# Re-laying the side work of a fused channel-attention and SwiGLU kernel over its pipeline steps

## The chip, the cores and the metric

The kernel runs on one core of one Trainium2 chip. The metric is device time in microseconds (us), from three timed runs before the change: 1446.28, 1451.61 and 1455.15, median 1451.61. A profile shows one further execution of 1448.67 us, whose span from the first to the last instruction is 1446.8 us. Engines are named as in the profile: PE is the matrix engine (PEld its weight loads), DVE the vector engine, ACT the scalar engine, POOL is GpSimd, SP issues the DMAs.

## What is computed

Two batches of 6016 rows and 256 channels go through a channel attention; its output, read as 12032 tokens of 256, goes through a gated feed-forward layer of width 1536.

```python
qn = q / (norm(q, axis=1) + 1e-06);  kn = k / (norm(k, axis=1) + 1e-06)
s = kn.transpose(0, 2, 1) @ qn / tau
a = exp(s - s.max(-1)); a /= a.sum(-1) + 1e-09     # "quotients"
x = (v @ a).reshape(12032, 256)
xn = x / sqrt(mean(x * x, -1) + 1e-06) * rms_g
g = xn @ w_gate;  silu = g / (1 + exp(-g))
out = (silu * (xn @ w_val)) @ w_out
```

## The kernel before

All matrix products of the feed-forward part are kept near fp32 accuracy by splitting each operand into a high part (rounded to a shorter type, "hi", made on ACT) and a low part (the rest, "lo", a subtraction on DVE or POOL), and adding three products: hi·hi, hi·lo, lo·hi.

The 12032 tokens are worked off in 24 blocks j = 0 to 23 of up to 512 tokens, each block in 12 steps f = 0 to 11 of 128 hidden columns. Blocks 2 to 22 use a Winograd form of Strassen's scheme, seven products for eight. The seven products of step (j, f) are spread over three calls of `emit_step`: numbers 5 and 1 in the step itself, 3 and 6 one step later, 7, 2 and 4 two steps later. So in each step PE does products 7 and 2 of two steps ago (tiles `pu`, `pq`), 3 and 6 of the step before, 5 and 1 of this step, then the first half of an output job (`po`, five steps late), product 4 of two steps ago, and the second half of the output job. A step's `pu` tile is one of three; its `pq` is the only one.

The chain behind the products runs over two steps. In an even step DVE adds the gate products (L801, L802), ACT makes the Silu (L817, L835); in the odd step DVE adds the value products (L801, L802), multiplies (L820, then L829 after product 4), ACT makes the hi part `gx` (L734) and POOL its lo part (L740). For column pairs 1 to 4 of a block ("turned" pairs) DVE then makes four differences in place in the same tile `zg` (`run_turned`, L726), in the next even step, once POOL has read it; one step later ACT and POOL make `gy` and `gz` from the differences.

Output jobs of a block accumulate in four banks `po0` to `po3`. `po2` lies in the bank of pool `ps_m`, `po3` in that of `ps_s`; the two halves of the attention product `px` of a later block use the same two banks.

Beside this main chain, each block j carries side work for other blocks, which three tables lay over its steps: `steady` (after the step), `steady_mid` (inside the step, before the output halves) and `steady_pre` (before the Silu or the multiply). `turn4`, `turn3`, `turn2` are the same for blocks 4, 3 and 2. Within an engine the order is the order in which the code is written; each engine works its own list strictly in that order. The names in the tables:

- for block j-1: `copy` (ACT, one accumulator's copy, L1011), `sums_` (DVE, four adds, L1021), `c0`, `c1` (DVE, L1030), `store` (DVE transposes, L1041, and four DMAs);
- for block j+1: `scale` (ACT, L558, waits for 16 DMAs issued after `m1`), `parts` (POOL, L571 and L576), `xh0`, `xh1` (ACT, hi parts, L600), `xl0`, `xl1` (DVE, lo parts, two instructions each, L612);
- for block j+2: `v1` (DVE transposes, L427), `vh1`, `vl1` (hi and lo of v, L443, L448), `x0`, `x1` (PE, `px`, L459), `q0`, `q1` (ACT squares, L475), `r0`, `r1` (POOL, two small instructions, L484 and L488), `n0`, `n1` (ACT, L500, reads `px` and `r`'s result and so sets its bank free), `m0`, `m1` (DVE transposes, L539; behind `m1` the 16 DMAs on SP, L548);
- for block j+3: `load` (4 DMAs), the first half's transposes, hi (`split_v_high`) and later lo (`vl0`).

Of the kernel before, what the change touches and what calls it, by code (L numbers as in the profile page):

```python
# [12 lines left out]
ALU = mybir.AluOpType  # L13
# [6 lines left out]
def kernel(  # L20
# [17 lines left out]
    nc = tc.nc  # L38
# [3 lines left out]
    KC = C // P  # L42
# [6 lines left out]
    STRA = 4  # L49
# [43 lines left out]
    def f32(ap):  # L93
        return ap.bitcast(F32)
# [210 lines left out]
    def softmax_div(b, c):  # L305
        if c == 0:
            a_hl[b] = []
            for i in range(2):
                a_hl[b].append(sm_p.tile([P, KC, C], F32R, tag=f"a{i}", name=f"a{i}_{b}"))
                if b == i == 0:  # L310
                    sm_p.tile([P, 8], F32, tag="apart", name="apart")
        ah, al = a_hl[b]
        z, mx = sm_t[b]
        s = mx[:, KC + c:KC + c + 1]
        nc.vector.tensor_scalar(out=s, in0=s, scalar1=1e-9, scalar2=None, op0=ALU.add)
        nc.vector.reciprocal(s, s)
# [23 lines left out]
    B1 = NB // B  # L340
# [219 lines left out]
    def emit_xT_parts(j):  # L560


        if j == NB - 1:
            return
        h = blocks[j][2] * P // 2
        x = moved[j]
        new_xT(j)
        t = xn_p.tile([P, 4, HN], F32, tag="moved", name=f"xp_{j}")
        moved[j] = (x, t)
        a2, b2 = (x[:, 1, i * h:(i + 1) * h] for i in range(2))  # L570
        nc.gpsimd.tensor_tensor(  # L571
            out=t[:, 0:3:2, :h], in0=x[:, :, h:2 * h],
            in1=x[:, 0, :2 * h].rearrange("p (i n) -> p i n", i=2), op=ALU.subtract,
        )
        for o, i0 in ((1, b2), (3, a2)):
            nc.gpsimd.tensor_tensor(out=t[:, o, :h], in0=i0, in1=t[:, o - 1 if o == 1 else 1, :h], op=ALU.subtract)  # L576

    def xT_round(j, i):

        h = blocks[j][2] * P // 2  # L580
        slots = ((0, 1), (1, 3)) if i == 0 else ((3, 5), (5, 7))
        hi, lo = ([y[:, a:b] for a, b in slots] for y in xp[j])
        if i == 0:
            x = [moved[j][0][:, c, :2 * h].rearrange("p (i n) -> p i n", i=2) for c in range(KC)]
            src = [x[0][:, :1], x[1]]
        else:
            src = [moved[j][1][:, m:m + 2, :h] for m in (0, 2)]
        return src, hi, lo

    def emit_xT_high(j, i):  # L590
        if j == NB - 1:
            if i == 0:
                new_xT(j)
                nc.scalar.activation(
                    out=xT[j][0], in_=moved[j][:, :, :blocks[j][2] * P], func=AF.Copy
                )
            return
        src, hi, _ = xT_round(j, i)
        for o, x in zip(hi, src):
            nc.scalar.activation(out=o, in_=x, func=AF.Copy)  # L600

    def emit_xT_low(j, i, engine=nc.vector):
        if j == NB - 1:
            if i == 0:
                nc.vector.tensor_tensor(
                    out=xT[j][1], in0=moved[j][:, :, :blocks[j][2] * P], in1=f32(xT[j][0]),
                    op=ALU.subtract,
                )
            return
        src, hi, lo = xT_round(j, i)  # L610
        for o, x, y in zip(lo, src, hi):
            engine.tensor_tensor(out=o, in0=x, in1=f32(y), op=ALU.subtract)  # L612

    def emit_xT_round(j, i):
        emit_xT_high(j, i)
# [38 lines left out]
    def build_so(k, piece):  # L654
        p = PAIRS[k]
        if piece == 0:
            t = s_tmp["so", k] = pool["wk"].tile([P, 4, 2 * P], F32, tag="wk", name=f"wo_{k}")
            nc.vector.tensor_tensor(
                out=t[:, :2], in0=f32(wo[0][:, 2 * p:2 * p + 2]), in1=f32(wo[1][:, 2 * p:2 * p + 2]),
                op=ALU.add,  # L660
            )
            a12, a22, a11, a21 = (t[:, i, e * P:(e + 1) * P] for i in range(2) for e in range(2))
            s1, s2, s3, s4 = (t[:, 2 + i, e * P:(e + 1) * P] for i in range(2) for e in range(2))
            for o, i0, i1, op in (
                (s1, a21, a22, ALU.add), (s2, s1, a11, ALU.subtract),
                (s3, a11, a21, ALU.subtract), (s4, a12, s2, ALU.subtract),
            ):
# [386 lines left out]
    with tc.manual_schedule():  # L1054
# [42 lines left out]
        for i in range(nch):  # L1097
            n = chunks[0][i][1]
# [89 lines left out]
        def at(j, f, go):  # L1188
            extra.setdefault((j, f), []).append(go)
# [75 lines left out]
            at(STRA - 1 + f // NF, f % NF, lambda k=k, i=i: build_so(k, i))  # L1265
        at(STRA, 7, last_so)
        for i in range(3):
            at(STRA, 7 + i, lambda i=i: build_so(3, i))

        at(3, 1, lambda: inverse_norms(1))  # L1270
        at(3, 2, lambda: spread_norms(1, ps_m, "m"))
# [1 line left out]
        at(3, 5, lambda: softmax_min(1, 0))  # L1273
        at(3, 6, lambda: softmax_min(1, 1))
        at(7, 4, lambda: (softmax_exp(1, 0), softmax_exp(1, 1)))
        at(B1 - 2, 2, lambda: softmax_div(1, 0))
        at(B1 - 2, 3, lambda: softmax_div(1, 1))

        steps = [(j, f) for j in range(NB) for f in range(NF)]
        owed = []  # L1280
# [49 lines left out]
        vh0, vl0, vh1, vl1 = (of(2, lambda n, go=go, h=h: go(n, h)) for h in range(2) for go in (split_v_high, split_v_low))  # L1330
        xh0, xl0, xh1, xl1 = (of(1, lambda n, go=go, i=i: go(n, i)) for i in range(2) for go in (emit_xT_high, emit_xT_low))

        steady = {
            0: (scale, vl0),
            1: (xh0, v1),
            2: (sums_, xl0),
            3: (vh1, xh1),
            4: (c0, c1, vl1),
            5: (store, xl1),
            6: (n0,),  # L1340
            7: (r1, load),
            8: (m0,),
            10: after(3, vm(0)),
            11: after(3, lambda n: split_v_high(n, 0)),
        }
        steady_mid = {1: (parts,), 2: (copy,), 4: (x0, q0, r0), 6: (x1, q1)}
        steady_pre = {8: (n1,), 9: (m1,)}
        turn4 = {
            **steady,
            0: (vl0,),  # L1350
            1: (scale, v1),
            2: (xh0,),
            3: (xl0, xh1),
            4: (vh1, c0, c1),
            5: (vl1,),
            6: (store, n0, xl1),
        }
        turn4_mid = {**steady_mid, 1: (), 2: (parts,), 4: (lambda j: build_so(2, 2), x0, q0, r0)}
        turn3 = {
            3: (v0,),  # L1360
            4: (c0, c1, scale, s0),
# [2 lines left out]
            7: (s1,),  # L1364
            8: (rest, load),
            9: (n0,),
            10: (r1,),
            11: (m0, m1, *after(3, vm(0)), *after(3, lambda n: split_v_high(n, 0))),
        }
        turn3_mid = {5: (parts,), 7: (x0, q0, r0), 9: (x1, q1), 11: (n1,)}  # L1370
        turn2_mid = {**turn3_mid, 0: after(1, xn(1)), 5: ()}
# [4 lines left out]
            5: (scale,),  # L1376
            6: (parts, hi, v1),
            8: (rest,),
            11: (m0, m1),
        }  # L1380
        turn1 = {
            0: after(1, vs(1), sq(0), rr(0)),
# [22 lines left out]
        }  # L1405
        ends = (turn0, turn1, turn2, turn3, turn4, steady)
        mids = ({}, {}, turn2_mid, turn3_mid, turn4_mid, steady_mid)
        pres = ({}, {}, {}, {}, steady_pre, steady_pre)

        def emit_all(o):  # L1410
            go = emit_out(*o)
# [77 lines left out]
```

## Time and profile before

| | before |
|---|---|
| median of three runs | 1451.61 us |
| profiled execution, its span | 1448.67 us, 1446.8 us |
| PE busy, share of the span | 1310.4 us, 91% |
| DVE, ACT, POOL busy | 985.3 us (68%), 857.2 us (59%), 653.2 us (45%) |
| mean granted PE clock | 0.976 of full speed |
| block 13 (one of the like blocks 5 to 20), its length | 58.28 us |

PE is busy 91% of the span, but its ends are modelled, and a busy PE may run at half its clock. So a block is best read by its length, by where PE's idle time stands in it, and by the clock there.

### The profile page before, as it was taken

What the parts mean: (1) busy time and instruction counts of PE and PEld (TensorE: products, weight loads), DVE (VectorE), ACT (ScalarE), POOL (GpSimd) and SP (SyncE); (2) the same over time, 40 slices, a digit from 0 to 9 for tenths busy, and PEclk for the clock granted to TensorE, in tenths of its full rate; (3) what the DMA queues carried; (4) which work ended last, traced back from release to release, by engine and by line L of the source; (5) the groups of instructions that cost most, each with busy time, mean ns of one, the idle gap of its engine ahead of it and who ended that gap; (6) DMA issues with size and microseconds to landing.
All of it is one profiled execution on the core that took longest, in us unless ns stands there. A gap on an engine that the chain in (4) does not pass through costs nothing.

```text
span 1446.8 us, 25348 instructions
## 1 busy us (share of the span) xinstructions
PE 1310.4 (91%) x9312; PEld 1225.9 (85%) x9312; DVE 985.3 (68%) x1746; ACT 857.2 (59%) x1765; POOL 653.2 (45%) x531
## 2 busy tenths in 40 slices
PE   9999999988898888988889889898898898988999
PEld 7899899978798787887888879888788798887998
DVE  5799786668667756667666666776666666766663
ACT  5566566666555665655556655566565555565652
POOL 0210466645454454444545445446354554454450
PEclk9999999999999999999999999999999999999999
DMA  8975311202102111021020210211102102111121
GB/s 290 309 238 153 95 44 29 32 15 45 30 16 43 23 24 30 15 45 30 15 35 14 41 30 16 43 22 25 31 15 45 30 16 39 21 27 16 25 60 27
DMA packets 229373, 75.98 MB, mean 53 GB/s; under 512 B 186880, under 2 KB 220800, under 8 KB 229248
## 3 DMA queue, kind: packets, MB, share of 16 engines
q1 hardware_dynamic: 228416, 73.12, 21.3%
q8 instruction: 73, 1.20, 0.3%
q10 hardware_dynamic: 832, 1.25, 0.3%
q14 instruction: 52, 0.43, 0.1%
HBM read 48.50 MB, written 14.42 MB: 43 GB/s over the span
## 4 chain that ended last, share of the span: by engine, by line
PE 26%; ACT 11%; DVE 9%; POOL 9%; issue 5%; SPq 4%; DMA 1%; DVEq 0%; POOLq 0%; ACTq 0%
PE pu L772 12%; PE po L996 9%; POOL gz L740 4%; SPq L548 4%; DVE xt L612 4%; POOL gx L740 2%; ACT t L813 2%; ACT zg L817 2%; PE pq L772 2%; POOL gy L740 1%; ACT xn L475 1%; PE px L459 1%; DVE zg L801 1%; ACT xnT L558 1%; DMA xnT<-xw 1%
## 5 line engine op out<-in xcount | busy, mean ns | idle before, releaser
L772 PE MATMUL pu<-xt,w 128*128 128x256 f32 x2268 | 401.4, 286 | 22.0 <-DVE zv L801 16.6
L772 PE MATMUL pu<-xt,s 128*128 128x256 f32 x2268 | 366.3, 286 | 20.2 <-ACT zg L835 10.7
L772 PEld LDWEIGHTS pu<-xt,w 128*128 128x128 f32 x2268 | 330.2, 192 | 47.4 <-DVE zv L801 29.1
L772 PEld LDWEIGHTS pu<-xt,s 128*128 128x128 f32 x2268 | 316.6, 192 | 42.4 <-ACT zg L835 18.4
L740 POOL TENSOR_TENSOR gy<-zg,gy 128x512 fp32r<-128x512 f32 x126 | 172.1, 1366 | 282.1 <-ACT gy L734 239.1
L740 POOL TENSOR_TENSOR gx<-zg,gx 128x768 fp32r<-128x768 f32 (+1 forms) x126 | 205.5, 1631 | 207.9 <-ACT gx L734 129.8
L813 ACT ACTIVATE t<-pu 128x512 f32<-128x512 f32 x252 | 151.1, 600 | 176.0 <-DVE zg L802 80.5
L996 PE MATMUL po<-gx,w 128*128 128x256 f32 (+1 forms) x984 | 191.5, 315 | 0.0
L726 DVE TENSOR_TENSOR zg<-zg 128x256 f32<-128x256 f32 x304 | 129.0, 424 | 88.3 <-POOL gx L740 80.5
L808 ACT ACTIVATE t<-pu 128x256 f32<-128x256 f32 x252 | 96.1, 381 | 99.0 <-PE pu L772 98.6
L734 ACT ACTIVATE gx<-zg 128x768 fp32r<-128x768 f32 (+1 forms) x126 | 96.0, 762 | 83.9 <-DVE zg L829 61.2
L996 PEld LDWEIGHTS po<-gx,w 128*128 128x128 f32 x984 | 141.0, 189 | 4.5
L820 DVE TENSOR_TENSOR zg<-zg,zv 128x768 f32<-128x768 f32 x126 | 135.8, 1078 | 10.0 <-ACT zg L817 0.3
L801 DVE TENSOR_TENSOR zv<-pu,t 128x512 f32<-128x512 f32 x126 | 85.8, 681 | 70.2 <-PE pu L772 56.3
L772 PE MATMUL pq<-xt,w 128*128 128x256 f32 x756 | 132.6, 285 | 0.0
L996 PE MATMUL po<-gy,so 128*128 128x256 f32 x342 | 68.9, 315 | 64.4 <-ACT xn L500 64.4
L801 DVE TENSOR_TENSOR zg<-pu,t 128x512 f32<-128x512 f32 x126 | 86.4, 686 | 46.5 <-POOL gz L740 30.9
L740 POOL TENSOR_TENSOR gz<-zg,gz 128x512 fp32r<-128x512 f32 x76 | 116.2, 1528 | 0.0
L996 PEld LDWEIGHTS po<-gy,so 128*128 128x128 f32 x342 | 55.7, 215 | 68.1 <-ACT xn L500 68.1
L772 PEld LDWEIGHTS pq<-xt,w 128*128 128x128 f32 x756 | 110.1, 194 | 0.0
L817 ACT ACTIVATE zg<-zg 128x768 f32<-128x768 f32 x126 | 105.8, 840 | 0.0
L185 PE MATMUL s<-raw 128*128 128x256 f32 x376 | 87.3, 386 | 3.2 <-DMA raw<-in_k_dram 3.2
(173 smaller groups left out, 2204.9 us busy)
## 6 DMA issues: line engine op xcount, KB each, us to landing
v<-in_v_dram SPq DMA_DIRECT2D x84, 128.0 KB, 3.8
xnT<-xw SPq DMA_DIRECT2D x336, 32.0 KB, 1.9
out_dram<-ob SPq DMA_DIRECT2D x84, 128.0 KB, 3.3
raw<-in_q_dram SPq DMA_DIRECT2D x20, 512.0 KB, 5.0
raw<-in_k_dram SPq DMA_DIRECT2D x19, 512.0 KB, 6.4
wraw<-in_moe_w_gate_dram SPq DMA_DIRECT2D x12, 256.0 KB, 5.3
wraw<-in_moe_w_val_dram SPq DMA_DIRECT2D x12, 256.0 KB, 5.5
wraw<-in_moe_w_out_dram SPq DMA_DIRECT2D x12, 256.0 KB, 5.7
```

Source lines behind the costliest of these rows:

```text
L185: nc.tensor.matmul(out=s_ps[b][:, c, :], lhsT=r[:, 1, t, c * P:(c + 1) * P], rhs=r[:, 0, t, :], start=(t0 + t == 0 and c == 0), stop=(t0 + ...
L548: nc.sync.dma_start(out=x[S * i:S * (i + 1), :, a * n * S:(a + 1) * n * S], in_=w[S * a:S * (a + 1), :, i, :n, :].rearrange("p c t s -> p ...
L726: nc.vector.tensor_tensor(out=z[:, o], in0=z[:, i0], in1=z[:, i1], op=ALU.subtract)
L734: nc.scalar.activation(out=gh, in_=hh, func=AF.Copy)
L740: engine.tensor_tensor(out=gl, in0=hh, in1=f32(gh), op=ALU.subtract)
L772: nc.tensor.matmul(out=out, lhsT=wm[wi], rhs=xm[xi], start=(start and q == 0), stop=(q == 2), skip_group_check=True,)
L801: nc.vector.tensor_tensor(out=z[:, 1:], in0=u, in1=t[:, :2], op=ALU.add)
L808: nc.scalar.activation(out=mt[:, 0], in_=mu[:, 1], func=AF.Copy)
L813: nc.scalar.activation(out=nt[:, 1:], in_=nu, func=AF.Copy)
L817: nc.scalar.activation(out=zg[:, 1:], in_=zg[:, 1:], func=AF.Silu)
L820: nc.vector.tensor_tensor(out=zg[:, 1:], in0=zg[:, 1:], in1=z, op=ALU.mult)
L996: nc.tensor.matmul(out=acc[b][:, o:o + g.shape[-1]], lhsT=w, rhs=g, start=first, stop=True, skip_group_check=True,)
```

## The change

The tables are laid anew for blocks from 4 on. The halves of `px` and what follows them (`x`, `q`, `r`, `n`) stand a step earlier, and `n1` two steps; `copy` stands behind step 2 instead of inside it; `scale`, `xl0`, `vl1` and `store` move into the middle of later steps; `xh1` goes from behind step 3 to behind step 5, and `xl1`, two instructions behind step 5, is split into one inside step 7 and one behind it. In block 4 the side work moves further (its `scale` from behind step 1 into step 3, `n1` into step 8), and a weight preparation of that block goes two steps later. The first half's hi part moves ahead of `gx` in step 11. Batch 1's quotients (`softmax_div`) are made behind steps 9 and 11 of block 9 instead of 2 and 3 of block 10. `new_xT` is called where the first hi part is made. No arithmetic instruction is added or dropped.

```diff
-        new_xT(j)                       # emit_xT_parts
 ...
     def emit_xT_high(j, i):
+        if i == 0:
+            new_xT(j)
 ...
-    def emit_xT_low(j, i, engine=nc.vector):
+    def emit_xT_low(j, i, engine=nc.vector, part=None):
 ...
+        for k, (o, x, y) in enumerate(zip(lo, src, hi)):
+            if part in (None, k):
+                engine.tensor_tensor(out=o, in0=x, in1=f32(y), op=ALU.subtract)
 ...
-            at(STRA, 7 + i, lambda i=i: build_so(3, i))
+            at(STRA, 9 + i, lambda i=i: build_so(3, i))
 ...
-        at(B1 - 2, 2, lambda: softmax_div(1, 0))
-        at(B1 - 2, 3, lambda: softmax_div(1, 1))
+        at(B1 - 3, 9, lambda: softmax_div(1, 0))
+        at(B1 - 3, 11, lambda: softmax_div(1, 1))
 ...
+        xl1a, xl1b = (of(1, lambda n, k=k: emit_xT_low(n, 1, part=k)) for k in range(2))
         steady = {
-            0: (scale, vl0),
+            0: (vl0,),
             1: (xh0, v1),
-            2: (sums_, xl0),
-            3: (vh1, xh1),
-            4: (c0, c1, vl1),
-            5: (store, xl1),
-            6: (n0,),
-            7: (r1, load),
+            2: (copy, sums_),
+            3: (vh1,),
+            4: (c0, c1),
+            5: (xh1,),
+            7: (xl1b, load),
             8: (m0,),
             10: after(3, vm(0)),
-            11: after(3, lambda n: split_v_high(n, 0)),
         }
-        steady_mid = {1: (parts,), 2: (copy,), 4: (x0, q0, r0), 6: (x1, q1)}
-        steady_pre = {8: (n1,), 9: (m1,)}
+        steady_mid = {
+            1: (scale,),
+            2: (parts, xl0),
+            3: (x0, q0, r0),
+            4: (vl1, n0),
+            5: (x1, q1, r1),
+            6: (n1, store),
+            7: (xl1a,),
+            9: (m1,),
+            11: after(3, lambda n: split_v_high(n, 0)),
+        }
```

On POOL, block 14, from the lo part of pair 0's second half (`gy1_14_1`) in step 5 on; `ss` and `rr` of `16_1` are `r1`, on which `n1` waits. Before:

```order
L740 TENSOR_TENSOR gy1_14_1_10149<-zg_14_0_10068,gy0_14_1_10148 128x512
L740 TENSOR_TENSOR gx1_14_2_10259<-zg_14_2_10169,gx0_14_2_10258 128x768
L740 TENSOR_TENSOR gy1_14_3_10261<-zg_14_2_10169,gy0_14_3_10260 128x512
L740 TENSOR_TENSOR gz1_14_3_10263<-zg_14_2_10169,gz0_14_3_10262 128x512
L740 TENSOR_TENSOR gx1_14_4_10379<-zg_14_4_10287,gx0_14_4_10378 128x768
L484 TENSOR_SCALAR ss_16_1_10322<-ss_16_1_10322 128x2
L488 TENSOR_TENSOR rr_16_1_10391<-ss_16_1_10322,mhalf_100 128x2
```

Of the change:

```order
L742 TENSOR_TENSOR gy1_14_1_10169<-zg_14_0_10064,gy0_14_1_10168 128x512
L484 TENSOR_SCALAR ss_16_1_10262<-ss_16_1_10262 128x2
L488 TENSOR_TENSOR rr_16_1_10266<-ss_16_1_10262,mhalf_100 128x2
L742 TENSOR_TENSOR gx1_14_2_10278<-zg_14_2_10187,gx0_14_2_10277 128x768
L742 TENSOR_TENSOR gy1_14_3_10280<-zg_14_2_10187,gy0_14_3_10279 128x512
```

`r1` has moved ahead of four lo parts, from behind step 7's `gx` to before step 5's.

On DVE, block 14, from the differences of pair 1 (step 6) to the second multiply of pair 3 (step 9). Before:

```order
L726 TENSOR_TENSOR zg_14_2_10169<-zg_14_2_10169 128x256 x4
L801 TENSOR_TENSOR zv_14_5_10350<-pu_14_5_10220,t_14_5_10221 128x512
L802 TENSOR_TENSOR zv_14_5_10350<-pq_14_5_10346,t_14_5_10221 128x256
L820 TENSOR_TENSOR zg_14_4_10287<-zg_14_4_10287,zv_14_5_10350 128x768
L829 TENSOR_TENSOR zg_14_4_10287<-pu_14_5_10220,zg_14_4_10287 128x256
L801 TENSOR_TENSOR zg_14_6_10407<-pu_14_6_10278,t_14_6_10279 128x512
L802 TENSOR_TENSOR zg_14_6_10407<-pq_14_6_10403,t_14_6_10279 128x256
L726 TENSOR_TENSOR zg_14_4_10287<-zg_14_4_10287 128x256 x4
```

Of the change:

```order
L728 TENSOR_TENSOR zg_14_2_10187<-zg_14_2_10187 128x256 x4
L1043 STREAM_TRANSPOSE ob_13_10323<-os_13_10104 128x16x32 x2
L803 TENSOR_TENSOR zv_14_5_10353<-pu_14_5_10220,t_14_5_10221 128x512
L804 TENSOR_TENSOR zv_14_5_10353<-pq_14_5_10349,t_14_5_10221 128x256
L822 TENSOR_TENSOR zg_14_4_10299<-zg_14_4_10299,zv_14_5_10353 128x768
L614 TENSOR_TENSOR xt1_15_10049<-xp_15_10082,xt0_15_10048 128x512
L831 TENSOR_TENSOR zg_14_4_10299<-pu_14_5_10220,zg_14_4_10299 128x256
L614 TENSOR_TENSOR xt1_15_10049<-xp_15_10082,xt0_15_10048 128x512
L803 TENSOR_TENSOR zg_14_6_10409<-pu_14_6_10290,t_14_6_10291 128x512
L804 TENSOR_TENSOR zg_14_6_10409<-pq_14_6_10405,t_14_6_10291 128x256
L728 TENSOR_TENSOR zg_14_4_10299<-zg_14_4_10299 128x256 x4
```

The two transposes of `store` and both instructions of `xl1` now stand between one turned pair's differences and the next one's; `m0` and `m1` (L539) follow as before.

On ACT, block 14, step 2: the Silu of pair 0, and `copy` (`os_13`). Before:

```order
L813 ACTIVATE t_14_2_10060<-pu_14_2_10059 128x512
L817 ACTIVATE zg_14_0_10068<-zg_14_0_10068 128x768
L1011 ACTIVATE os_13_10086<-po2_13_9691 128x256
L835 ACTIVATE zg_14_0_10068<-pu_14_0_9948 128x256
L734 ACTIVATE gy0_13_11_10046<-zg_13_10_9957 128x512
```

Of the change:

```order
L815 ACTIVATE t_14_2_10056<-pu_14_2_10055 128x512
L819 ACTIVATE zg_14_0_10064<-zg_14_0_10064 128x768
L837 ACTIVATE zg_14_0_10064<-pu_14_0_9948 128x256
L1013 ACTIVATE os_13_10104<-po2_13_9695 128x256
L736 ACTIVATE gy0_13_11_10040<-zg_13_10_9957 128x512
```

The copy now stands behind the second Silu, and on PE behind step 2's whole output job.

## Rows read from the trace of the kernel before

**Rows 1.** Waits of the whole run: engine, line, waited for; total us, times, longest.

```profile
PE po L996 <- ACT xn L500: 64.4, 18, 4.7
PE po L996 <- ACT os L1011: 21.4, 19, 2.3
PE pu L772 <- DVE zv L801: 16.6, 36, 1.7
```

**Rows 2.** Windows, blocks 4, 13, 22, then a stretch inside block 13.

```profile
core 0: us, PE busy (x) PEld busy (x) DVE busy (x) ACT busy (x) POOL busy (x), PEclk, DMA share, GB/s
290.85:352.16 61.31, 52.04 (x371) 48.87 (x369) 46.11 (x90) 36.99 (x82) 28.18 (x22) 0.94 0.17 33
...
822.70:880.98 58.28, 51.71 (x387) 48.60 (x385) 38.57 (x73) 34.43 (x73) 28.64 (x23) 0.97 0.15 28
1345.65:1392.85 47.20, 45.77 (x362) 44.18 (x361) 32.37 (x62) 29.85 (x56) 25.98 (x17) 1.00 0.18 42
867.30:870.70 3.40, 3.40 (x19) 3.40 (x18) 0.40 (x1) 1.42 (x3) 1.34 (x2) 0.50 0.00 0
```

**Rows 3.** Timeline of block 13, step 8: start, us, engine, instruction, idle before it.

```profile
862.31 1.84 POOL L740 TENSOR_TENSOR gx<-zg,gx 128x768 fp32r<-128x768 f32 x1
...
864.77 0.87 POOL L488 TENSOR_TENSOR rr<-ss,mhalf 128x2 f32<-128x2 f32 x1
865.68 0.84 ACT L500 ACTIVATE xn<-px,rr 128x256 f32<-128x256 f32 x2 [1.54 <-POOL rr L488]
866.57 0.76 PE L996 MATMUL po<-gy,so 128*128 128x256 f32 x4 [3.54 <-ACT xn L500]
```

**Rows 4.** Timeline of block 13, PE in step 6.

```profile
853.15 1.57 PE L459 MATMUL px<-a,vt 128*128 128x256 f32 x12
854.56 0.86 PE L996 MATMUL po<-gy,w 128*128 128x512 f32 x3
```

**Rows 5.** Timeline, two turned pairs in a row, blocks 13 and 14.

```profile
873.32 0.42 DVE L829 TENSOR_TENSOR zg<-pu,zg 128x256 f32<-128x256 f32 x1 [0.54 <-PE pu L772]
...
876.64 1.80 DVE L726 TENSOR_TENSOR zg<-zg 128x256 f32<-128x256 f32 x4 [1.44 <-POOL gx L740]
...
878.36 0.76 DVE L427 STREAM_TRANSPOSE vw<-v 128x256 f32<-128x256 f32 x2
...
881.60 0.41 DVE L829 TENSOR_TENSOR zg<-pu,zg 128x256 f32<-128x256 f32 x1
...
886.66 0.68 DVE L448 TENSOR_TENSOR vt<-vw,vt 128x512 fp32r<-128x512 f32 x1
...
888.00 0.64 PE L772 MATMUL pu<-xt,w 128*128 128x256 f32 x3 [0.24 <-DVE zv L801]
...
889.26 0.42 DVE L829 TENSOR_TENSOR zg<-pu,zg 128x256 f32<-128x256 f32 x1
```

**Rows 6.** DVE groups by form in block 13: count, busy us, mean ns, idle before.

```profile
L820 DVE TENSOR_TENSOR zg<-zg,zv 128x768 f32<-128x768 f32 x7 | 7.8, 1121 | 0.6
...
L539 DVE STREAM_TRANSPOSE xw<-xn 128x512 f32<-128x512 f32 x2 | 1.4, 707 | 0.6 <-ACT xn L500 0.6
...
L612 DVE TENSOR_TENSOR xt<-xnT,xt 128x512 fp32r<-128x512 f32 x1 | 0.7, 689 | 0.0
```

**Rows 7.** Timeline, narrow windows: POOL and DVE at 852 us.

```profile
852.06 1.84 POOL L740 TENSOR_TENSOR gx<-zg,gx 128x768 fp32r<-128x768 f32 x1 [1.25 <-ACT gx L734]
...
852.15 2.30 DVE L612 TENSOR_TENSOR xt<-xp,xt 128x512 fp32r<-128x512 f32 x1
```

**Rows 8.** Timeline, the DMAs of `xnT` and `scale`, block 13, then block 4.

```profile
872.03 11.17 SPq L548 DMA_DIRECT2D xnT<-xw  x16
885.14 1.34 ACT L558 ACTIVATE xnT<-xnT,g_sb 128x512 f32<-128x512 f32 x2
...
303.99 1.33 ACT L558 ACTIVATE xnT<-xnT,g_sb 128x512 f32<-128x512 f32 x2 [4.46 <-DMA xnT<-xw]
```

**Rows 9.** Timeline, block 14, step 2: what PE waits for.

```profile
893.33 0.39 PE L996 MATMUL po<-gz,so_dg 128*128 128x256 f32 x1 [1.05 <-ACT os L1011]
```

More of the change, by code (lines that the diff above doesn't have):

```diff
@@ L583, in xT_round @@
         if i == 0:
-            x = [moved[j][0][:, c, :2 * h].rearrange("p (i n) -> p i n", i=2) for c in range(KC)]
+            whole = moved[j][0] if isinstance(moved[j], tuple) else moved[j]
+            x = [whole[:, c, :2 * h].rearrange("p (i n) -> p i n", i=2) for c in range(KC)]
             src = [x[0][:, :1], x[1]]
@@ L590, in emit_xT_high @@
     def emit_xT_high(j, i):
+        if i == 0:
+            new_xT(j)
         if j == NB - 1:
             if i == 0:
-                new_xT(j)
                 nc.scalar.activation(
@@ L610, in emit_xT_low @@
         src, hi, lo = xT_round(j, i)
-        for o, x, y in zip(lo, src, hi):
-            engine.tensor_tensor(out=o, in0=x, in1=f32(y), op=ALU.subtract)
+        for k, (o, x, y) in enumerate(zip(lo, src, hi)):
+            if part in (None, k):
+                engine.tensor_tensor(out=o, in0=x, in1=f32(y), op=ALU.subtract)
     def emit_xT_round(j, i):
@@ L1331 @@
         xh0, xl0, xh1, xl1 = (of(1, lambda n, go=go, i=i: go(n, i)) for i in range(2) for go in (emit_xT_high, emit_xT_low))
+        xl1a, xl1b = (of(1, lambda n, k=k: emit_xT_low(n, 1, part=k)) for k in range(2))
         steady = {
-            0: (scale, vl0),
+            0: (vl0,),
             1: (xh0, v1),
-            2: (sums_, xl0),
-            3: (vh1, xh1),
-            4: (c0, c1, vl1),
-            5: (store, xl1),
-            6: (n0,),
-            7: (r1, load),
+            2: (copy, sums_),
[3 more added lines that the diff above has]
+            7: (xl1b, load),
             8: (m0,),
             10: after(3, vm(0)),
+        }
[8 more added lines that the diff above has]
+            9: (m1,),
             11: after(3, lambda n: split_v_high(n, 0)),
         }
-        steady_mid = {1: (parts,), 2: (copy,), 4: (x0, q0, r0), 6: (x1, q1)}
-        steady_pre = {8: (n1,), 9: (m1,)}
         turn4 = {
             **steady,
[L1350 to L1353, printed above, removed]
+            0: (vh0,),
+            1: (vl0,),
+            2: (),
+            3: (xh0, v1),
             4: (vh1, c0, c1),
-            5: (vl1,),
-            6: (store, n0, xl1),
-        }
-        turn4_mid = {**steady_mid, 1: (), 2: (parts,), 4: (lambda j: build_so(2, 2), x0, q0, r0)}
+        }
+        turn4_mid = {
+            **steady_mid,
+            1: (),
+            2: (),
+            3: (scale,),
+            4: (lambda j: build_so(2, 2), parts, xl0, x0),
+            5: (vl1, q0, r0),
+            6: (n0, x1, q1, r1, store),
+            8: (n1,),
+        }
         turn3 = {
@@ L1366 @@
             9: (n0,),
-            10: (r1,),
-            11: (m0, m1, *after(3, vm(0)), *after(3, lambda n: split_v_high(n, 0))),
+            10: (r1, *after(3, vm(0))),
+            11: (m0, m1),
         }
@@ L1378 @@
             8: (rest,),
-            11: (m0, m1),
+            10: (r1,),
         }
@@ L1407 @@
         mids = ({}, {}, turn2_mid, turn3_mid, turn4_mid, steady_mid)
-        pres = ({}, {}, {}, {}, steady_pre, steady_pre)
+        pres = ({}, {}, {}, {}, {}, {})
         def emit_all(o):
```

## The prediction

> **What bounds the kernel now.** I read the waits first: PE stands 64.4 us in all at `po`, 18 times, waiting for ACT's L500, and 21.4 us, 19 times, for the copy L1011 [rows 1]. Both are once a block. Then the windows by block: block 13 takes 58.28 us, and PE's granted clock in it is 0.97 [rows 2]. What PE needs comes from its undisturbed stretches: twelve products of 256 columns go from 853.15 to 854.56, 0.1175 us each [rows 4]. A block has 252 products, 24 of `px` and 84 of output at 256 columns, and 24 of output at 512, which I take as twice as long: 360 x 0.1175 + 24 x 0.235 = 47.9 us. Block 22, without the 24 of `px`, would need 45.1; PE is busy 45.77 there and the block takes 47.20 [rows 2], so the floor holds. Of block 13's 58.28 us, 10.4 are therefore lost.
>
> The timeline says where. In step 8 the small `rr` on POOL stands behind a `gx` of 1.84 us; ACT's `n1` starts only at 865.68, and PE, which needs the bank for `po3`, stands 3.54 us [rows 3]. Right behind it the granted clock is 0.50 for 3.40 us [rows 2], so half of that, 1.7 us, is lost too: 5.2 us a block for one wait. The copy costs 1.1 (21.4 / 19). The other 4.1 us are short stops in steps 1 and 3 to 7, the `zv` wait among them (16.6 us over 36 times, two a block) [rows 1].
>
> **n1.** In the new order `r1` stands ahead of step 5's `gx` on POOL and `n1` in the middle of step 6. The bank is wanted in step 8, two steps of some 3.7 us later (31 to 33 products x 0.1175), so the wait goes: 5.2 us a block. In exchange `gx` of step 5 can start up to 0.9 us later (`rr`, 0.87 [rows 3]); it also waits for ACT's `gx0` behind the same squares, and I count nothing.
>
> **copy.** Behind step 2 it no longer stands in the way of the output job: 1.1 us saved [rows 1, 9]. But `px` of step 3 now needs that bank, after the copy and DVE's first add. From the end of step 2's job to `px` PE has 18 products, 2.1 us; a copy and an add of 256 columns are each near the 0.42 of L829 [rows 5]. It fits unless ACT is late, and ACT has `scale` (1.34 [rows 8]) in step 1 now, ahead of `gx` and `xh0`, and arrives in step 2 about 1 us later than before. I take 0.3 us, with bounds of 0 and 2.0.
>
> **The short stops.** `store` and `xl1` leave step 5, the squares leave the even steps, where they stood ahead of the second Silu, and `px` no longer follows a late DVE in step 4. I count the 3.6 us of steps 3 to 7 as gone. The 0.5 in step 1 belongs to the next part.
>
> **What comes in.** The chain of a turned pair runs from one L829 to the next: ACT `gx`, POOL `gx`, DVE's four differences (they wait for POOL), the side work there, L801, L802, L820, L829. Two measured rounds: 881.60 - 873.32 = 8.28 us with 0.76 of side work in it, 889.26 - 881.60 = 7.66 with 0.68 [rows 5]. Bare, that is 7.52 and 6.98, in the mean 7.25. PE needs 63 products, 7.40 us, for the same two steps. So a bare round just fits, and side work between the differences and L829 adds to the time in full. Before, the stop in step 8 let DVE catch up in every block; that rest is now gone. There are four such rounds in a block:
>
> - round 1 (steps 6, 7): two transposes of `store`, 0.7 each as those of L539, and one `xl1` instruction, 0.69 [rows 6]: 7.25 + 1.4 + 0.69 = 9.34;
> - round 2 (steps 8, 9): `m0` and `m1`, 0.71 each: 8.67. The second `xl1` instruction lies beside `gx` on ACT and POOL (2.7 us) and costs nothing; if that cover is gone, 0.69;
> - round 3 (steps 10, 11): 8.28 as measured; round 4 (steps 0, 1): 7.66 as measured.
>
> The sum is 33.95 against 29.6 for PE: 4.35 us behind. PE has some slack: the two measured rounds are 0.88 and 0.26 over, and PE then stands 0.24 [rows 5], so it stops when DVE is some 0.9 behind. 3.45 us are left. One more thing lies on this chain: an L612 that starts beside a POOL instruction took 2.30 us instead of 0.69 [rows 6, 7], 1.6 more, and `xl1`'s first half now stands where POOL works on `gy` and `gz`. I take half of that, 0.8. Loss of the rounds: 4.2 us, with bounds of 1.5 (side work falls into DVE's idle time) and 7.5 (two such waits more).
>
> In steps 2 to 5 no turned pair runs, so the backlog is worked off before the next block's step 6.
>
> **DMAs.** The 16 DMAs of `xnT` take SP 11.17 us and `scale` can start some 13 us after `m1` [rows 8]. From `m1` to the new `scale` in the middle of step 1 PE alone needs 14 us; nothing is counted. `store`'s and `load`'s eight DMAs stand ahead on SP, issued two steps before `m1`; if they run late there, `scale` waits as in block 4.
>
> **The rest.** Block 4 waits 4.46 us for `xnT` before `scale` [rows 8] and loses 0.06 x 61.31 = 3.7 us to the clock [rows 2]; with `scale` in step 3 that wait goes, while its `n1`, only in step 8, still stops PE for some 2.5 us: 8 us saved, bounds 3 and 12. Block 21 has the wait of 3.5 us too, but less side work to gain from, and I count 3.5; block 22 has the copy's wait alone, 1.2. The quotients are the same DVE work at another busy place: 0, give or take 2.
>
> **Sum.** A block goes from 58.28 to 47.9 + 4.2 + 0.3 = 52.4, 5.9 less, times 16 for blocks 5 to 20: 94. With 8 + 3.5 + 1.2 it is 107 us off the profiled 1448.67: 1342. The median of the runs lay 2.94 above the profiled one, so **1345 us**.
>
> **Rivals.**
>
> *The rounds hide (0.16).* For it: DVE is busy 38.57 of 58.28 us [rows 2], so it has room. Against: the chain is one of waits, not of load. A loss of 1.8 us gives 49.7 a block, 8.6 x 16 + 12.7 = 150 less: 1302 with the median's offset.
>
> *The bank of `px` (0.16).* ACT comes late in step 2, copy and add follow late, and `px` in step 3 waits 2 us in each block, which sends DVE later into the rounds (5 us). 47.9 + 7 = 54.9: 3.4 x 16 + 12.7 = 67 less, 1385.
>
> *Slower: DVE and POOL shut each other out (0.06).* Eight DVE instructions a block in these places read two operands that both lie beside POOL's: four L820, two of `xl0`, two of `xl1`. Each that meets a POOL instruction costs 1.6 us [rows 6, 7], on the chain. Without any the new loss is 3.75; the old one is 10.4; it decides from more than four of the eight. Six would make 3.75 + 9.6 = 13.4, a block of 61.3, 3.0 x 16 - 12.7 = 35 more: 1487. Against it: the seven L820 of block 13 take 1.12 us in the mean [rows 6], so few of them meet one now. The Trainium skill, page "SBUF — State Buffer", section "Who interferes with whom", has this as a rule: a DVE instruction with two SBUF inputs and a GpSimd instruction that reads SBUF exclude each other, and the second to issue blocks until the first is done. The trace agrees: the POOL instruction ends at 852.06 + 1.84 = 853.90, and the DVE one 0.55 us later. By that rule alone, applied to all eight, the sum would be 3.75 + 13 = 16.7 us a block and the kernel slower; the trace shows it for the few that meet.
>
> *The change does not reach the wait (0.04).* `n1` waits in step 6 for something else and ACT, in order, holds everything: about 1440. The order on POOL speaks against it.
>
> **Chances.** Forecast 0.58 (1322 to 1372), rivals as given. A measurement of this kernel can tell 1% from no change. Faster by over 1%: 0.58 + 0.16 + 0.16 = 0.90. Within 1%: 0.04. Slower: 0.06. The range takes in the first two rivals' values: **1305 to 1395**, leaving the last two and the edges out.
>
> **What would show it.** After the change the waits of PE for L500 should be gone but for block 4's, and those for the copy too; the clock should be full from block 5 to 22; PE should stop briefly in steps 7 to 1 for DVE's L801 or L829 (their new lines), and the interval between the L829 of steps 7 and 9 should be near 8.7 us. It is wrong if PE still stands in step 8 for ACT, if `px` in step 3 waits for DVE, or if DVE's two-operand instructions are often over 2 us.

## The result, and the profile after

The change takes 1347.3 us in the median of four runs (1346.63 to 1349.69), against 1452.78 (1446.28 to 1455.15) for the kernel before beside it: a ratio of 0.928, with a 95% interval of 0.925 to 0.932. The forecast was 1345 us, between 1305 and 1395. The profiled execution took 1349.69 us, its span 1347.7, with a mean granted clock of 0.996. The lines of the code moved by two (L820 is now L822, L829 is L831, L801 is L803, L612 is L614).

The busy times on the page of the change:

```profile
PE 1272.7 (94%) x9312; PEld 1205.9 (89%) x9312; DVE 1037.1 (77%) x1746; ACT 854.0 (63%) x1765; POOL 646.7 (48%) x531
```

DVE is busy 52 us longer than before with the same 1746 instructions. PE's waits answer to [rows 1]:

```profile
PE pu L774 <- DVE zv L803: 40.6, 50, 1.6
PE pu L774 <- DVE zg L831: 17.7, 34, 1.0
PE po L998 <- ACT xn L500: 2.7, 1, 2.7
```

The wait for `n1` is left once, in block 4, and the one for the copy is gone. What PE waits for now is DVE. By block, as in [rows 2]: blocks 4, 5, 14 and 22.

```profile
290.60:346.78 56.18, 51.58 (x371) 49.14 (x370) 46.79 (x84) 36.56 (x83) 26.88 (x22) 0.94 0.19 36
346.78:401.63 54.85, 50.91 (x387) 48.80 (x385) 43.13 (x76) 34.29 (x74) 30.30 (x24) 0.97 0.16 28
...
827.61:880.67 53.06, 49.45 (x387) 47.32 (x385) 41.79 (x73) 34.34 (x75) 28.17 (x24) 1.00 0.18 31
1250.51:1296.05 45.54, 45.54 (x362) 44.14 (x361) 32.23 (x63) 29.95 (x57) 25.59 (x17) 1.00 0.20 46
```

The granted clock is full from block 6 on. Block 5 is not yet like the others: the weight preparation that the change moves to step 11 of block 4 (three L680) holds DVE from 347.79 to 351.00 us, where it took 0.8 us before, PE then stands 1.88 us for DVE's L803, and behind that stop the clock is 0.50 for 3.4 us. DVE takes 41.79 us for the work of block 14; in block 13 before, the same work took 38.57. Where a block's time went shows in its steps (us from the first product of one step to that of the next, block 14, read from PE's timeline):

| step | 0 | 1 | 2 | 3 | 4 | 5 | 6 | 7 | 8 | 9 | 10 | 11 |
|---|---|---|---|---|---|---|---|---|---|---|---|---|
| before | 3.91 | 4.05 | 5.18 | 4.69 | 5.72 | 4.76 | 5.84 | 3.87 | 8.84 | 3.91 | 3.91 | 3.54 |
| after | 3.99 | 5.36 | 3.88 | 5.27 | 3.86 | 5.27 | 3.86 | 3.64 | 4.72 | 4.26 | 4.62 | 4.33 |
| `a_rounds` (below) | 3.91 | 3.54 | 3.88 | 5.27 | 3.86 | 5.27 | 3.86 | 3.53 | 3.91 | 3.54 | 3.91 | 3.54 |

`px` adds 1.41 to the steps that hold it (4 and 6 before, 3 and 5 after). Steps 2 to 6 lose nothing now; all of the loss against the 47.9 us that PE needs, 5.1 us, lies in steps 7 to 1, where the turned pairs run. Their rounds are read from one L831 to the next; DVE and POOL in block 14's steps 5 to 11 and block 15's steps 0 and 1:

```profile
854.81 0.42 DVE L831 TENSOR_TENSOR zg<-pu,zg 128x256 f32<-128x256 f32 x1 [1.29 <-PE pu L774]
...
861.79 1.29 POOL L742 TENSOR_TENSOR gz<-zg,gz 128x512 fp32r<-128x512 f32 x1
862.20 1.70 DVE L822 TENSOR_TENSOR zg<-zg,zv 128x768 f32<-128x768 f32 x1
...
864.42 0.41 DVE L831 TENSOR_TENSOR zg<-pu,zg 128x256 f32<-128x256 f32 x1
...
870.67 1.30 POOL L742 TENSOR_TENSOR gz<-zg,gz 128x512 fp32r<-128x512 f32 x1
871.18 1.60 DVE L822 TENSOR_TENSOR zg<-zg,zv 128x768 f32<-128x768 f32 x1
...
873.33 0.38 DVE L831 TENSOR_TENSOR zg<-pu,zg 128x256 f32<-128x256 f32 x1
...
879.55 1.29 POOL L742 TENSOR_TENSOR gz<-zg,gz 128x512 fp32r<-128x512 f32 x1
880.12 1.53 DVE L822 TENSOR_TENSOR zg<-zg,zv 128x768 f32<-128x768 f32 x1
881.58 0.41 DVE L831 TENSOR_TENSOR zg<-pu,zg 128x256 f32<-128x256 f32 x1
...
884.91 1.80 DVE L728 TENSOR_TENSOR zg<-zg 128x256 f32<-128x256 f32 x4 [1.99 <-POOL gx L742]
886.59 1.29 POOL L742 TENSOR_TENSOR gy<-zg,gy 128x512 fp32r<-128x512 f32 x1 [1.72 <-ACT gy L736]
886.63 1.80 DVE L448 TENSOR_TENSOR vt<-vw,vt 128x512 fp32r<-128x512 f32 x1
...
889.46 0.96 DVE L822 TENSOR_TENSOR zg<-zg,zv 128x768 f32<-128x768 f32 x1
890.34 0.42 DVE L831 TENSOR_TENSOR zg<-pu,zg 128x256 f32<-128x256 f32 x1
```

The rounds take 9.61, 8.91, 8.25 and 8.76 us. In three of them L822 begins while POOL still works on `gz` and takes 1.53 to 1.70 where it needs 0.96 (889.46): the first `gz` ends at 863.08, L822 at 863.90. In the fourth it is L448 (`vl0`): 1.80 where [rows 5] have 0.68. It begins 0.04 us behind POOL's `gy` and ends 0.55 behind it, the distance of [rows 7]. So an instruction counts as busy while it waits: over the run L822 takes 25.9 us more than before, L448 27.8 and `xl0` 32.7, `xl1` 24.5 less.

Why `vl0` was not held up before, the kernel before shows at the same place (DVE, ACT and POOL in the two rounds of [rows 5]):

```profile
880.13 1.55 DVE L820 TENSOR_TENSOR zg<-zg,zv 128x768 f32<-128x768 f32 x1
...
886.38 0.63 ACT L734 ACTIVATE gy<-zg 128x512 fp32r<-128x512 f32 x1
...
887.13 1.36 POOL L740 TENSOR_TENSOR gy<-zg,gy 128x512 fp32r<-128x512 f32 x1 [2.23 <-ACT gy L734]
...
888.38 0.96 DVE L820 TENSOR_TENSOR zg<-zg,zv 128x768 f32<-128x768 f32 x1
888.45 2.05 POOL L740 TENSOR_TENSOR gz<-zg,gz 128x512 fp32r<-128x512 f32 x1
```

There ACT was on `scale` until 886.48 [rows 8] (885.14 + 1.34), so `gy` came 0.47 behind L448's start. The change moved `scale` to step 1, ACT makes `gy` earlier, POOL's `gy` now comes 0.04 ahead of L448, and L448 waits for all of it. This is read from the two traces; no run moves `scale` alone.

### The profile page after: what moved, and what is told of

It is laid out like the page before. It is cut to its first block, busy times and chain, and to the rows that moved or that the text cites. A ratio compares the mean times of both kernels' runs of the same rounds, so it can differ in the third digit from the quotient of the medians.

```text
span 1347.7 us, 25377 instructions
## 1 busy us (share of the span) xinstructions
PE 1272.7 (94%) x9312; PEld 1205.9 (89%) x9312; DVE 1037.1 (77%) x1746; ACT 854.0 (63%) x1765; POOL 646.7 (48%) x531
## 4 chain that ended last, share of the span: by engine, by line
PE 66%; DVE 15%; POOL 6%; DMA 4%; issue 4%; SPq 2%; ACT 2%; DVEq 0%; ACTq 0%; POOLq 0%
PE pu L774 30%; PE po L998 16%; POOL gx L742 6%; PE px L459 5%; DVE zg L728 4%; PE pq L774 4%; PE pg L891 3%; PE s L185 3%; PE pv L891 3%; PE po L944 3%; DVE zv L803 2%; DMA raw<-in_k_dram 2%; DVE vt L448 2%; SPq L548 2%; DVE xw L539 2%
## 5 line engine op out<-in xcount | busy, mean ns | idle before, releaser
L774 PEld LDWEIGHTS pu<-xt,w 128*128 128x128 f32 x2268 | 326.7, 189 | 64.9 <-DVE zv L803 51.3
L774 PE MATMUL pu<-xt,s 128*128 128x256 f32 x2268 | 362.4, 284 | 18.9 <-DVE zg L831 17.7
L742 POOL TENSOR_TENSOR gy<-zg,gy 128x512 fp32r<-128x512 f32 x126 | 165.8, 1316 | 227.1 <-ACT gy L736 214.1
L822 DVE TENSOR_TENSOR zg<-zg,zv 128x768 f32<-128x768 f32 x126 | 161.7, 1283 | 12.4 <-DVE zv L804 0.9
L742 POOL TENSOR_TENSOR gz<-zg,gz 128x512 fp32r<-128x512 f32 x76 | 111.5, 1467 | 0.0
L803 DVE TENSOR_TENSOR zg<-pu,t 128x512 f32<-128x512 f32 x126 | 85.3, 677 | 32.4 <-PE pu L774 22.5
L736 ACT ACTIVATE gy<-zg 128x512 fp32r<-128x512 f32 x126 | 80.5, 639 | 46.6 <-DVE zg L728 45.4
L774 PEld LDWEIGHTS pq<-xt,w 128*128 128x128 f32 x756 | 107.4, 190 | 0.0
L803 DVE TENSOR_TENSOR zv<-pu,t 128x512 f32<-128x512 f32 x126 | 84.2, 669 | 15.9 <-ACT zg L837 7.6
L998 PE MATMUL po<-gy,w 128*128 128x512 f32 x300 | 85.4, 393 | 0.0
```

The source lines that it names most:

```text
L736: nc.scalar.activation(out=gh, in_=hh, func=AF.Copy)
L742: engine.tensor_tensor(out=gl, in0=hh, in1=f32(gh), op=ALU.subtract)
L774: nc.tensor.matmul(out=out, lhsT=wm[wi], rhs=xm[xi], start=(start and q == 0), stop=(q == 2), skip_group_check=True,)
L803: nc.vector.tensor_tensor(out=z[:, 1:], in0=u, in1=t[:, :2], op=ALU.add)
L822: nc.vector.tensor_tensor(out=zg[:, 1:], in0=zg[:, 1:], in1=z, op=ALU.mult)
L998: nc.tensor.matmul(out=acc[b][:, o:o + g.shape[-1]], lhsT=w, rhs=g, start=first, stop=True, skip_group_check=True,)
```

## The experiments

Three theories of what is left stood against each other. **Chain**: an instruction on DVE costs its time only if it stands between a pair's differences and the next L831; ahead of the differences, where DVE waits for POOL's `gx` anyway (1.99 us at 884.91), it is free. **Load**: DVE is merely busy, and the place does not matter. **Lock**: only the waits between DVE and POOL count. For what was removed: the stop for `n1` is worth its full length, or the rounds eat up what it gives. Ratios are to the kernel before, run on the same chip beside each. In the diffs ` ...` marks lines left out.

**`b_n1`: the kernel before with `n1` earlier, nothing else.**

```diff
-            7: (r1, load),
+            7: (load,),
 ...
-        steady_mid = {1: (parts,), 2: (copy,), 4: (x0, q0, r0), 6: (x1, q1)}
-        steady_pre = {8: (n1,), 9: (m1,)}
+        steady_mid = {1: (parts,), 2: (copy,), 4: (x0, q0, r0), 6: (x1, q1, r1), 7: (n1,)}
+        steady_pre = {9: (m1,)}
```

> The kernel before with one edit: the first square sums' two POOL instructions (r1) go from behind step 7 into step 6, and n1 from ahead of step 8's Silu into step 7. Chain theory: the wait with its half-clock stretch is 5.2 us of a block, 18 times; with the stop gone the four rounds of turned pairs run through (about 7.4 + 8.7 + 8.3 + 7.7 = 32.0 us against 29.6 for PE, 0.9 of slack), so about 1.5 us a block come in, 0.5 of which stand already: net 4.2 us a block, near 1377 us. Rival (the gain is spread over the many small moves, the wait is only where DVE's lateness shows): under 40 us, above 1412 us.

1379.53 us, ratio 0.951 (0.950 to 0.953): 70 of the 105 us, near the 1377 of the chain theory. The mean clock is 0.999. Steps 8 and 9 of block 13, the wait and the half clock behind it, fall from 12.79 to 7.64 together, 5.15 us; but step 11 rises from 3.54 to 4.34 and step 1 from 4.04 to 4.27, so the block loses only 3.76 us of its 58.28. The stop is worth its wait and its half clock, less what the rounds then lack. The short stops are apart from it: steps 2 to 6 of block 14 take 5.21, 4.68, 5.72, 4.78 and 5.83, as before.

**`b_copy`: the kernel before with the copy behind step 2.**

```diff
-            2: (sums_, xl0),
+            2: (copy, sums_, xl0),
 ...
-        steady_mid = {1: (parts,), 2: (copy,), 4: (x0, q0, r0), 6: (x1, q1)}
+        steady_mid = {1: (parts,), 4: (x0, q0, r0), 6: (x1, q1)}
```

> The kernel before with one edit: copy behind step 2, ahead of the four adds, instead of inside step 2. If the copy's wait is a loss of its own: 1.1 us a block, 19 times, some 20 us less, near 1432 us. Rival: PE comes to the next stop earlier and waits there (zv in step 3, or n1 in step 8): within 5 us of before.

1444.63 us, ratio 0.996 (0.995 to 0.998): 5 us, as the rival had it. In block 14 step 2 falls from 5.18 to 3.88, but step 3 rises from 4.69 to 5.78. Over the run PE's wait for the copy, 21.4 us, is gone, and its wait for L801 (`zv`) rises from 16.6 to 34.9. The timeline, DVE and PE from step 2 of block 14 on:

```profile
897.44 1.67 DVE L1021 TENSOR_TENSOR os<-po,os 128x256 f32<-128x256 f32 x4 [2.02 <-ACT os L1011]
...
899.03 1.61 DVE L612 TENSOR_TENSOR xt<-xnT,xt 128x256 fp32r<-128x256 f32 x2
900.56 0.68 DVE L801 TENSOR_TENSOR zv<-pu,t 128x512 f32<-128x512 f32 x1
...
901.29 0.64 PE L772 MATMUL pu<-xt,w 128*128 128x256 f32 x3 [1.64 <-DVE zv L801]
```

DVE waits 2.02 us for the copy, then has `sums_` and `xl0` ahead of L801, and PE stands for L801. In the change `xl0` moves too, from behind step 2 into its middle: to an earlier place, and not, like `scale` and `store`, to a later step. So it stands ahead of the copy's adds and fills that wait, and step 3 has no stop. No run moves the copy and `xl0` alone. DVE in the change:

```profile
839.21 2.91 DVE L614 TENSOR_TENSOR xt<-xnT,xt 128x256 fp32r<-128x256 f32 x2
...
842.04 1.66 DVE L1023 TENSOR_TENSOR os<-po,os 128x256 f32<-128x256 f32 x4
843.62 0.68 DVE L803 TENSOR_TENSOR zv<-pu,t 128x512 f32<-128x512 f32 x1
```

**`a_n1back`: the change with `r1` and `n1` at their old places.**

```diff
-            7: (xl1b, load),
+            7: (xl1b, r1, load),
 ...
-            5: (x1, q1, r1),
-            6: (n1, store),
+            5: (x1, q1),
+            6: (store,),
 ...
-        pres = ({}, {}, {}, {}, {}, {})
+        pres = ({}, {}, {}, {}, {}, {8: (n1,)})
```

> The changed kernel with r1 and n1 of blocks 5 on put back behind step 7 and ahead of step 8's Silu. Additive rival: the whole 5.2 us a block come back, 17 times, near 1435 us. Chain theory: the stop comes back but DVE catches up in it, so most of the 5.1 us that a block now loses in steps 7 to 1 goes; net 1.5 to 2.5 us a block more, 1373 to 1390 us.

Left out is a line that keeps block 4 as it was. The run takes 1409.05 us, ratio 0.972 (0.970 to 0.975): 62 us above the change. Neither number was met. The stop is longer than before, in its waits and in the stretch at half clock behind it (block 13):

```profile
PE po L998 <- ACT xn L500: 74.2, 18, 4.2
```

```profile
842.63:847.95 5.32, 5.31 (x25) 5.32 (x26) 1.76 (x3) 2.11 (x4) 2.00 (x2) 0.50 0.43 66
```

PE waits 4.24 us there (3.54 in the kernel before) and then runs 5.3 us at half clock, which loses half of that: 6.9 us where I had put down 5.2. The block takes 57.13 us instead of 53.07, 4.06 more, so 2.8 of the 6.9 come back in the rounds; over blocks 5 to 20 it is 3.0 a block in the mean. So the stop lets DVE catch up, as the chain theory has it and by about as much; what I had too low is the stop itself.

**`a_rounds`: the side work moved out of the rounds.** From block 5 on `store` and `xh1` stand behind step 4, `xl1` behind steps 5 and 7, `m0`, `m1` and the first half's transposes `vm(0)` ahead of the differences of steps 8 and 10, `vl0` behind step 11.

```diff
-            0: (vl0,),
-            4: (c0, c1),
-            5: (xh1,),
+            4: (c0, c1, store, xh1),
+            5: (xl1a,),
-            8: (m0,),
-            10: after(3, vm(0)),
+            11: after(3, lambda n: split_v_low(n, 0)),
 ...
+        steady_pre = {8: (m0, m1), 10: after(3, vm(0))}
 ...
-            6: (n1, store),
-            7: (xl1a,),
-            9: (m1,),
+            6: (n1,),
 ...
-        pres = ({}, {}, {}, {}, {}, {})
+        pres = ({}, {}, {}, {}, {}, steady_pre)
```

> The changed kernel with the side work of the rounds put elsewhere, none dropped: store behind step 4, xh1 behind step 4, xl1's halves behind steps 5 and 7, m0 and m1 ahead of step 8's differences, the first half's transposes ahead of step 10's, vl0 behind step 11 (blocks 5 on). Chain theory: what costs is not the work but its place between the differences and L831; DVE stands 1.3 to 2.0 us a round for POOL's gx just ahead of the differences, and the work fits there; the rounds fall to 7.3 to 7.6 us and a block to 48.5 to 49.5: 1275 to 1295 us. Rival (DVE, busy 77% of the span, is simply loaded): within 10 us of 1347.

The lines left out keep block 4 as it was. The run takes 1269.79 us, ratio 0.876 (0.874 to 0.877), below the 1275 to 1295 that the chain theory gave. A block takes 48.03 us, and PE is busy for all of them; block 14:

```profile
787.08:835.11 48.03, 48.03 (x386) 46.98 (x385) 40.07 (x73) 35.01 (x73) 31.35 (x24) 1.00 0.19 34
```

DVE ahead of the differences in steps 8 and 10:

```profile
822.80 1.29 DVE L539 STREAM_TRANSPOSE xw<-xn 128x512 f32<-128x512 f32 x2
824.02 1.75 DVE L728 TENSOR_TENSOR zg<-zg 128x256 f32<-128x256 f32 x4
...
829.90 0.76 DVE L427 STREAM_TRANSPOSE vw<-v 128x256 f32<-128x256 f32 x2
831.04 1.80 DVE L728 TENSOR_TENSOR zg<-zg 128x256 f32<-128x256 f32 x4 [0.38 <-POOL gx L742]
```

In the change DVE stood 1.38 and 1.99 us ahead of these differences, waiting for POOL; now it is 0 and 0.38. With its 73 instructions all still there, in a shorter block, DVE is no bound: the load theory falls. With the work the waits for POOL leave the rounds too (L822 takes 0.96 in rounds 2 to 4 now); the next three runs take the two apart.

**`a_vl0`: the change with `vl0` alone moved**, from behind step 0 to behind step 11.

```diff
-            0: (vl0,),
+            11: after(3, lambda n: split_v_low(n, 0)),
```

> The changed kernel with one instruction a block moved: vl0 (L448) from behind step 0, on the chain behind the differences, to behind step 11, where POOL stands idle. Chain theory with the exclusion of DVE and POOL: its own 0.68 us and the 1.12 it waits there for POOL (1.80 in the trace) both leave round 4; step 1, now 1.85 us over, comes down by 1.6 to 1.8, 17 times: 1317 to 1320 us. Rival, only the wait for POOL counts: 19 us less, near 1328. Rival, DVE is loaded: within 5 us of 1347.

1324.28 us, ratio 0.915 (0.913 to 0.917). The block falls from 53.06 to 51.35. L448 takes 0.67 there, and the fourth round ends at 873.41, 7.06 us after the third:

```profile
866.35 0.41 DVE L831 TENSOR_TENSOR zg<-pu,zg 128x256 f32<-128x256 f32 x1
866.68 0.67 DVE L448 TENSOR_TENSOR vt<-vw,vt 128x512 fp32r<-128x512 f32 x1
...
873.41 0.41 DVE L831 TENSOR_TENSOR zg<-pu,zg 128x256 f32<-128x256 f32 x1
```

1.70 of the 1.80 us leave the round: the work and the lock's wait both count. Sixteen such blocks would make 27; but block 5 gains only 1.0, and block 10 gets 2.1 us longer (55.16). Behind `vl0` stand the quotients of block 9: one of their DVE instructions, L320, now runs beside a `gx` of POOL and takes 1.92 us instead of 0.48, PE stands 2.12, and the granted clock behind that is 0.50 for 3.4 us.

**`a_dup_post` and `a_dup_pre`: the change with the two transposes of `vm(0)` done twice**, in `a_dup_post` where they stand, between differences and L831, in `a_dup_pre` (from block 5 on) ahead of the differences. `twice` is the old function with the same transposes once more behind it. The diff of the first, then of the second, both without the text of `twice`, and the second without the line that keeps block 4 as in `a_dup_post`:

```diff
-            10: after(3, vm(0)),
+            10: after(3, twice),
```

```diff
-            10: after(3, vm(0)),
 ...
-        pres = ({}, {}, {}, {}, {}, {})
+        pres = ({}, {}, {}, {}, {}, {10: after(3, twice)})
```

> The changed kernel with the first half's two transposes behind step 10 done twice (the second writes the same values again), from block 4 on. Both theories: 0.8 us a block more on DVE, and it stands behind the differences, on the chain: 18 times 0.7 to 0.8, near 1360 us.

> The same doubled transposes, but from block 5 on ahead of step 10's differences, where DVE stands 1.99 us for POOL's gx. Chain theory: 1.6 us fit there, and the 0.8 of the single ones leave the chain: 17 times 0.7 less than the changed kernel, near 1335 us, though DVE does more than in it. Rival, DVE is loaded: as the other doubled kernel, near 1360 us.

The first takes 1346.83 us, ratio 0.930 (0.929 to 0.932): no change, and a miss of both theories as I had costed them. The trace has the reason; POOL and DVE in round 3:

```profile
869.84 0.38 DVE L831 TENSOR_TENSOR zg<-pu,zg 128x256 f32<-128x256 f32 x1
...
875.55 0.73 DVE L1341 STREAM_TRANSPOSE vw<-v 128x256 f32<-128x256 f32 x2
...
876.07 1.27 POOL L742 TENSOR_TENSOR gz<-zg,gz 128x512 fp32r<-128x512 f32 x1
...
877.29 0.96 DVE L822 TENSOR_TENSOR zg<-zg,zv 128x768 f32<-128x768 f32 x1
878.16 0.42 DVE L831 TENSOR_TENSOR zg<-pu,zg 128x256 f32<-128x256 f32 x1
```

L822 comes 0.66 later, when `gz` is all but done (877.34), and takes 0.96 instead of 1.53. The round is 8.32 us, as against 8.25: the doubled work fell into the lock's wait.

The second takes 1326.46 us, ratio 0.916 (0.915 to 0.918), with twice the transposes 21 us *less* than the change (18 by the ratios). DVE and POOL in round 3:

```profile
858.26 0.38 DVE L831 TENSOR_TENSOR zg<-pu,zg 128x256 f32<-128x256 f32 x1
...
860.17 0.72 DVE L1341 STREAM_TRANSPOSE vw<-v 128x256 f32<-128x256 f32 x2
861.56 1.81 DVE L728 TENSOR_TENSOR zg<-zg 128x256 f32<-128x256 f32 x4 [0.67 <-POOL gx L742]
...
864.40 0.96 DVE L822 TENSOR_TENSOR zg<-zg,zv 128x768 f32<-128x768 f32 x1
864.50 2.02 POOL L742 TENSOR_TENSOR gz<-zg,gz 128x512 fp32r<-128x512 f32 x1
865.28 0.42 DVE L831 TENSOR_TENSOR zg<-pu,zg 128x256 f32<-128x256 f32 x1
```

All four transposes fit into the wait for `gx`, which shrinks from 1.99 to 0.67. The round is 7.02 us, 1.23 less: 0.7 for the work and 0.57 for the lock, since L822 now begins ahead of `gz`. The block falls by the same 1.23, to 51.83. I had counted the 0.7 alone.

**`a_final`: `a_rounds` with batch 1's quotients earlier**, behind steps 5 and 6 of block 9 instead of 9 and 11.

```diff
-        at(B1 - 3, 9, lambda: softmax_div(1, 0))
-        at(B1 - 3, 11, lambda: softmax_div(1, 1))
+        at(B1 - 3, 5, lambda: softmax_div(1, 0))
+        at(B1 - 3, 6, lambda: softmax_div(1, 1))
```

> The kernel with the rounds re-laid, and batch 1's quotients behind steps 5 and 6 of block 9 instead of 9 and 11. In the re-laid kernel blocks 9 and 10 take 49.51 and 50.07 us against 48.03 of their neighbours; if that is the quotients on the chain, some 2 to 3.5 us less, near 1267 us; if they only move the stop, the same 1270.

1266.85 us, ratio 0.875 (0.873 to 0.877), the lowest of all and near the 1267 expected; that it beats `a_rounds` the intervals do not tell. In the profiles blocks 9 and 10 together take 97.69 us instead of 99.58.

## Why the prediction was right, step by step

- **Sum.** Profile against profile, 107 us were forecast and 99.0 came. Blocks 5 to 20 gave 85.2 (937.74 to 852.51) where 94 stood, block 4 gave 5.1 of 8, block 21 4.5 for 3.5, block 22 1.65 for 1.2; 2.3 came behind block 22 and were not followed up. Block 10, where the quotients stood (put at 0), fell by 7.42 and block 14 by 5.18; 1.2 of the 2.2 more lies in step 3, behind the quotients (5.86 before, against 4.69). The forecast profile was 1342 and the profile 1349.69; that the medians differ by 2.3 alone is chance, since the runs of after lie below their profiled one and I had put the median above it.
- **Floor.** 47.9 us was right: `a_rounds` runs at 48.03.
- **n1.** The wait and the half clock behind it went, as the step says. The size was right too: 5.15 us in `b_n1`. That run shows the mechanism by itself, and that a stop's worth is not its length: of the 5.15, 1.4 come back in other steps.
- **copy and px.** No stop in step 3: 0 where 0.3 was counted. The copy's wait went too, but the 1.1 us are not the worth of its move: `b_copy` makes it alone and a like block falls by only 0.2 (5 us over the run). By the traces it takes `xl0` ahead of the adds as well, which the sum did not name.
- **Short stops.** Gone, and of their own worth, since `b_n1` leaves them standing. By the steps of block 14, against `a_rounds`, those of steps 3 to 7 were 3.1 us, for 3.6. Which of the moves takes away which of them no run shows; that part of the account is argued.
- **Rounds.** Here the size was off: 5.1 us for 4.2. Rounds 1 to 3 were 9.61, 8.91 and 8.25 for 9.34, 8.67 and 8.28. The 0.8 put down for `xl1` beside POOL came to nothing (0.68 and 0.67 us for its two instructions), which by chance covers part of what follows. The step that failed is "round 4 (steps 0, 1): 7.66 as measured": it takes 8.76. I read a duration from a round whose neighbour on ACT, `scale`, the change takes away; without it POOL's `gy` meets `vl0` (1.80 for 0.68). And the mean of two bare rounds, 7.25, hid the same lock: in the first of them L820 took 1.55, in the second 0.96, which is their whole difference of 0.54.
- **Block 4.** 5.1 for 8. The wait for `xnT` went, and that for `n1` is 2.7 us for the 2.5 put down. But the clock is 0.94 as before: two stretches at half clock of 3.4 us each have become one of 6.8 at that wait. And the sign "full from block 5" failed in block 5, which takes 54.85 us where a like block takes 53.1: the sum had nothing for the weight preparation moved to just ahead of it.
- **Rivals.** The rounds do not hide and `px` does not wait. DVE and POOL did shut each other out, five times among the eight instructions named (three L822, both of `xl0`) and at `vl0`, which I had not listed. By the count of the third rival, more than four of eight, the kernel would have been slower. But its price was wrong: an L822 lost 0.6 to 0.7 and not 1.6, and `xl0` lies where PE has time (step 2 loses nothing); so the kernel got faster all the same.

## What to carry to other kernels

On an engine that works in order, look at what stands just behind and just ahead of an instruction that waits for another engine: side work is free ahead of it as long as it fits into the wait, and behind it it lengthens the chain, unless another wait there takes it up, as in `a_dup_post`. Here the same instructions take 48.03 us a block laid one way and 53.06 the other, part of it work and part of it waits for POOL. A stop that is removed is worth its wait and the slow clock behind it, less the rest it gave to another chain; so after the edit read what had time to catch up there. And a duration read from the trace holds only as long as its neighbours on the other engines stay where they are.

## What was not expected of the hardware

- Whether a DVE instruction with two SBUF operands waits for a POOL instruction, or POOL for it, is decided by hundredths of a microsecond: 0.04 us behind POOL's start, L448 took 1.80 us, and 0.47 ahead of it 0.68. The sharpest pairs are an L820 of `b_n1` that starts 0.01 ahead of a `gy`, and an L822 of `a_rounds` that starts with a `gz`, less than 0.01 behind it:

```profile
1281.99 0.96 DVE L820 TENSOR_TENSOR zg<-zg,zv 128x768 f32<-128x768 f32 x1
1282.00 2.10 POOL L740 TENSOR_TENSOR gy<-zg,gy 128x512 fp32r<-128x512 f32 x1 [2.89 <-ACT gy L734]
```

```profile
355.17 1.29 POOL L742 TENSOR_TENSOR gz<-zg,gz 128x512 fp32r<-128x512 f32 x1
355.17 2.10 DVE L822 TENSOR_TENSOR zg<-zg,zv 128x768 f32<-128x768 f32 x1
```

- The Trainium skill, page "SBUF — State Buffer", section "Who interferes with whom", says that issue order decides who blocks. The traces agree in both directions: in the kernel before it was a `gz` that started 0.07 us behind an L820 (888.45 against 888.38) that took 2.05 us instead of 1.29.
- So more work on DVE can cost next to nothing: in `a_dup_post` some 0.7 us of added transposes lengthened a round by 0.07.
